# Nyström attention, feed-forward and top-1 experts on one core: another order of scores, sums and weights in the first batch

## The chip, the cores and the metric

The kernel runs on one core of a Trainium2 chip. The metric is the device time of one execution in microseconds (us). The core has five engines that run their own instruction streams in order: TensorE (PE, with its weight loads shown as PEld), VectorE (DVE), ScalarE (ACT), GpSimd (POOL) and SyncE (SP), whose queue issues nearly all DMAs. A change below 0.2% (some 2.5 us) can hardly be told from none.

## The reference, cut to what matters

```python
# q, k, v: (8, 8, 576, 64): 8 batches, 8 heads, 576 tokens; m = 32 landmarks, D = 64
q_lm = q.reshape(B, H, m, S // m, D).mean(axis=3)      # sums of 18 tokens
k_lm = k.reshape(B, H, m, S // m, D).mean(axis=3)
A  = sm(q, k_lm)          # sm: softmax of the scaled scores
Bm = sm(q_lm, k_lm)
C  = sm(q_lm, k)
Z  = Bm.transpose(0, 1, 3, 2) / (norm1 * norminf + 1e-06)
for _ in range(6):
    Z = 2 * Z - Z @ Bm @ Z
x = A @ Z @ C @ v                                      # then to (4608, 512)
h = np.maximum(x @ w_in, 0.0)                          # w_in 512 x 2048
x = (h * h) @ w_out                                    # w_out 2048 x 512
# then: logits, argmax, one of 8 experts for each token: relu(x @ w1[e]) @ w2[e], gated
```

## The kernel before

**Tiling.** A batch is 576 tokens, worked on in two halves of 288 (`c` = 0, 1). The attention's last factor Z·C·v is a matrix `wt` (128x128) of a batch, and instead of x the kernel forms G = wt · w_in (`gt`, tiles `gb`) in four rounds of 512 columns of w_in each (`chunk`, PE rows `bank<-wf,wt` or `two<-wf,wt`; `split_g` then makes a high and a low part, on ACT and DVE). `gemm(b)` runs for each half over 16 chunks `f` of the hidden layer: 6 matmuls `hp<-ab,gb` (128x288), then on ACT `r` = relu, `gh` = rounded square and `g` = square, on DVE `gl` = g - gh, and two chunks later (`second`) 12 matmuls `acc<-gh,wo` and `acc<-gl,wo`. Below, (0,0) is batch 0's first half, (0,1) its second, (1,0) batch 1's first half.

**Side work.** While `gemm(b)` runs, the attention of batch b+1 (`unit`: sums, transposes, landmarks, scores, softmax, powers of Z, wt) is woven between its matmuls at a rate from `RATES`. Batch 0's own unit (`u["early"]`) runs ahead of everything, with 8 of the weight pieces converted beside it. A scheduler sets the order of instructions in each queue from priorities; where the code says `follow`, an order is forced.

**Sums and landmarks.** Landmark sums (18 tokens each) are made from the loaded keys or queries `t`, four heads (`hg`) at a time. In batches 0 and 1 (`u["pe"]`) they are made on DVE (2 reduces), with a copy on POOL that doubles them, but batch 0's last group of queries is summed on POOL; in the other batches all is on POOL (`st`, `sums`). `landmarks` then transposes the doubled sums (128x128) on PE, two transposes for the keys and two for the queries of a batch.

**Weights.** w_in and w_out arrive as 8-byte floats, in 16 pieces each, 512 KB apiece (`raw`, SP's queue). A piece becomes 4-byte floats in steps: `m` (ACT for half of w_in's first pieces, POOL for the others), `r` (ACT), and two adds of halves on POOL (tiles `wf` for w_in, `w` for w_out). The order is all of w_in, then all of w_out. A w_in piece is also written back to memory (`win`), from where later batches read it (`wi`). A w_out piece is at once split into a high (ACT L218) and a low part (DVE L224) in its final tile `wo`; `w` has two buffers, so POOL's third piece waits for DVE's split of the first. The split cannot start before G has used the w_in piece, since `wo` takes over that piece's tile.

Of the kernel before, what the change touches and what calls it, by code (L numbers as in the profile page):

```python
# [23 lines left out]
LM = 32  # L24
# [16 lines left out]
CONV_BUFS = 2  # L41


CONV_EARLY = 14
CONV = 0.45
CONV_SOON = 0.8
CONV_FIRST = 2
# [5 lines left out]
RATES = {(0, 0): 0.3, (0, 1): 0.8}  # L53
# [4 lines left out]
G_STEPS = {7: 0, 10: 1, 13: 2, 15: 3}  # L58
# [34 lines left out]
class Kernel:  # L93
    def __init__(self, tc, ins, out):
# [7 lines left out]
        self.held = []  # L102
# [43 lines left out]
    def convert(self, jobs):  # L146
# [19 lines left out]
        def fetch(i):  # L166

            j, c = pieces[i]
            raw = pool.tile([128, 2 * W], I32, tag="raw", name="raw", bufs=RB)
            nc.sync.dma_start(  # L170
                out=raw.bitcast(U16)[:, 0:4 * W - 1], in_=jobs[j][0][:, c:c + W].bitcast(U16)[:, 1:4 * W]
            )
            st[i] = raw

        def scale(i):
# [56 lines left out]
    def convert_in(self):  # L232

        def job(i):
            n, kp = divmod(i, KD)

            def place():
                self.wf[i] = self.wop.tile([128, 2, 512], F32, tag=f"wo{i}", name="wf")[:, 0]
# [5 lines left out]
                lambda w: self.hold(lambda: self.nc.sync.dma_start(out=self.win_d[n][:, kp], in_=w)),  # L244
# [4 lines left out]
    def convert_out(self):  # L249

        def job(f):
            def parts(w):
                while self.g_done <= f // KD:
                    self.first_g_of(self.g_done)
                self.wo[f] = self.wop.tile([128, 2, DM], F32R, tag=f"wo{f}", name="wo")
                self.split(self.wo[f], w, self.nc.vector)

            return (
                self.w_out[f * 128:(f + 1) * 128, :],
                lambda: self.cv.tile([128, 512], F32, tag="cw", name="w", bufs=CONV_BUFS),  # L260
                parts,
# [3 lines left out]


# [150 lines left out]
    def load_next(self, pool=None):  # L417
# [7 lines left out]
        self.nc.sync.dma_start(  # L425
            out=t.rearrange("p s d -> p (s d)"), in_=src.rearrange("h (l s) d -> (h l) (s d)", s=SEG)
        )

    def load_v(self, b, g, pool=None):
        if b < B:  # L430
            t = self.vt[b, g] = (pool or self.ld).tile([PT, 4, R6 * D], F32, tag="v", name="v", bufs=1)
            src = self.v[b].rearrange("(a g i) (p r) d -> a g p i (r d)", g=2, i=2, r=R6)
            for a in range(2):
                self.nc.sync.dma_start(out=t[:, 2 * a:2 * a + 2], in_=src[a, g])

    def sums(self, u, nm, hg):

        if hg == 0:
            u[nm + "s"] = self.sm.tile([128, 2, 2, D], F32, tag=f"{nm}s", name="sums", bufs=1)
        s, t = u[nm + "s"][:, hg], self.qk[nm, u["b"], hg]  # L440
        if not u["pe"] or u["early"] and nm == "q" and hg == 1:
# [18 lines left out]
        self.nc.gpsimd.tensor_copy(out=s[:, 1], in_=s[:, 0])  # L460

    def transposed(self, u, nm, hg, i):

        if i == 0:
            u[nm, hg] = self.tp.tile([128, 4, 9, LM], F32, tag="xT", name="x", bufs=2)
# [11 lines left out]
        if i == 2 and not (u["b"] == 0 and nm == "q" and hg == 1):  # L477
            self.hold(self.load_next)
# [35 lines left out]
    def landmarks(self, u, nm):  # L514
        nc = self.nc
        pd = self.bank()
        with self.run_of():
            for hg in range(2):
                self.transpose(
                    pd[:, 128 * hg:128 * hg + 128], u[nm + "s"][:, hg].rearrange("p c d -> p (c d)"), self.ident  # L520
                )
# [272 lines left out]
    def last_values(self, u):  # L794
# [4 lines left out]
        for j in range(4):  # L799
            self.nc.vector.tensor_copy(out=self.crossed(wz, j), in_=w[32 * j:32 * j + 32])  # L800
# [26 lines left out]
    def unit(self, u):  # L827

        both = [(hg, i) for hg in range(2) for i in range(3)]
        if u["pe"]:  # L830
            self.sums(u, "k", 0)
            for hg, i in both:
                self.transposed(u, "k", hg, i)
                if (hg, i) == (0, 0):
                    self.sums(u, "k", 1)
                elif i == 2:
                    self.sums(u, "q", hg)
# [7 lines left out]
        for nm in "kq":  # L845
            self.landmarks(u, nm)
            yield STEP
# [35 lines left out]
        def a():  # L883
            yield STEP
            for i in range(2):
                self.scores_a(u, i)
                yield STEP
                yield STEP
# [677 lines left out]
```

## Time and profile before

| | us |
|---|---|
| median of 3 runs | 1260.96 |
| the runs | 1259.1 to 1261.58 |
| profiled execution | 1259.2 |
| its span | 1257.5 |
| PE busy | 1206.7 (96%) |
| DVE, ACT, POOL busy | 591.3, 615.2, 421.3 |

The profile is of one execution, 1.8 us below the median. It names for every instruction the line of the kernel (L402 is the helper that emits the big matmuls, L398 that for small ones, L410 transposes), the tile written and the tiles read. A window view gives how busy each engine was in a stretch and PEclk, the granted clock of TensorE as a share of its full speed (1.00 is 2.4 GHz, .50 is 1.2 GHz). Matmuls overlap in the timeline, so what one occupies is the distance from its start to the next one's start.

### The profile page before, as it was taken

The page shows a single profiled execution, that of the slowest core. Times are in us where ns is not written, and L with a number is a line of the kernel's source. Part 1 is how long each engine was busy: PE and PEld are TensorE (multiplying, and loading weights), DVE is VectorE, ACT ScalarE, POOL GpSimd, SP SyncE. Part 2 cuts the span into 40 slices and gives each one's busy share as a digit, 9 for nine tenths or more (in the row PEclk, how much of TensorE's full clock was granted, in tenths as well). Part 3 has the DMA queues.
Part 4 walks back from the last instruction along what each step waited for, and adds up shares of the span by engine and source line. Part 5 has one row for each costly group of instructions (what it writes and reads, how often), then busy time and mean ns, then how long its engine had stood idle before and what let it go on. Part 6 is the DMA issues. An engine that isn't in the chain of part 4 may idle for free.

```text
span 1257.5 us, 25149 instructions
## 1 busy us (share of the span) xinstructions
PE 1206.7 (96%) x9834; PEld 1078.6 (86%) x9834; DVE 591.3 (47%) x1498; ACT 615.2 (49%) x1433; POOL 421.3 (34%) x568
## 2 busy tenths in 40 slices
PE   4598999999999999999999999999999999999996
PEld 3377888989989989989989999998888888888885
DVE  5586466567547557556556332233333323323231
ACT  5586364564564564564564454553343433424331
POOL 5787514332233233232112000163342423424220
PEclk7699999999999999999999999999999999999998
DMA  9944333252152142141133210152534435343231
GB/s 339 336 164 135 124 122 109 91 168 61 59 171 64 53 158 77 53 158 58 54 120 108 69 37 2 39 151 84 143 105 139 129 115 159 108 125 110 90 96 40
DMA packets 88408, 142.24 MB, mean 113 GB/s; under 512 B 6430, under 2 KB 61758, under 8 KB 84702
## 3 DMA queue, kind: packets, MB, share of 16 engines
q1 hardware_dynamic: 87854, 139.97, 34.4%
q8 instruction: 79, 1.29, 0.4%
q0 software_dynamic: 288, 0.43, 0.1%
q14 instruction: 43, 0.35, 0.1%
q10 hardware_dynamic: 144, 0.20, 0.0%
HBM read 117.47 MB, written 23.11 MB: 112 GB/s over the span
## 4 chain that ended last, share of the span: by engine, by line
PE 90%; DVE 3%; DMA 3%; ACT 2%; POOL 1%; issue 1%; SPq 0%; POOLq 0%; ACTq 0%; DVEq 0%
PE acc L402 32%; PE hp L402 32%; PE y L402 17%; PE two L398 4%; PE bank L398 2%; PE bank L410 1%; DMA raw<-in_moe_w_in_dram 1%; PE pl L398 1%; DMA v<-in_v_dram 1%; PE pt L1168 1%; DVE x L488 1%; DMA t<-in_q_dram 1%; DVE gl L1079 1%; ACT r L185 0%; DVE ma L559 0%
## 5 line engine op out<-in xcount | busy, mean ns | idle before, releaser
L402 PE MATMUL acc<-gh,wo 128*128 128x288 f32 x2048 | 453.5, 299 | 7.7 <-ACT wo L218 5.0
L402 PEld LDWEIGHTS acc<-gh,wo 128*128 128x128 f32 x2048 | 341.1, 189 | 30.0 <-ACT gh L1077 8.4
L402 PE MATMUL acc<-gl,wo 128*128 128x288 f32 x1024 | 288.9, 298 | 1.1 <-DVE gl L1079 1.1
L402 PE MATMUL hp<-ab,gb 128*128 128x288 f32 x1536 | 255.7, 301 | 1.6 <-ACT r L1076 1.5
L402 PEld LDWEIGHTS hp<-ab,gb 128*128 128x128 f32 x1536 | 216.0, 189 | 21.3 <-issue 11.8
L1076 ACT ACTIVATE r<-hp 128x288 f32<-128x288 f32 x256 | 105.4, 412 | 256.0 <-PE hp L402 254.4
L1079 DVE TENSOR_TENSOR gl<-g,gh 128x288 fp32r<-128x288 f32 x256 | 131.4, 514 | 198.8 <-ACT g L1078 192.6
L402 PE MATMUL y<-s,h 128*128 128x512 f32 (+1 forms) x896 | 223.0, 396 | 0.8 <-ACT h L1311 0.5
L402 PEld LDWEIGHTS hp<-xs,s 128*128 128x128 f32 x1536 | 212.2, 188 | 7.5 <-DVE ls L1522 0.3
L402 PE MATMUL hp<-xs,s 128*128 128x288 f32 x1536 | 217.1, 295 | 0.2 <-DVE ls L1522 0.2
L402 PEld LDWEIGHTS acc<-gl,wo 128*128 128x128 f32 x1024 | 193.4, 189 | 4.0 <-DVE gl L1079 3.0
L402 PEld LDWEIGHTS y<-s,h 128*128 128x128 f32 (+1 forms) x896 | 160.6, 184 | 37.7 <-ACT h L1311 0.7
L230 POOL TENSOR_TENSOR s<-r,s 128x256 fp32r<-128x256 f32 x128 | 102.0, 819 | 234.8 <-ACT s L218 234.8
L1311 ACT ACTIVATE h<-hp 128x288 fp32r<-128x288 f32 x128 | 52.6, 412 | 186.8 <-PE hp L402 172.6
L1314 DVE SCALAR_TENSOR_TENSOR h<-hp,h 128x64 fp32r<-128x64 f32 (+2 forms) x192 | 62.6, 354 | 166.3 <-ACT h L1311 165.9
L1077 ACT ACTIVATE gh<-r 128x288 fp32r<-128x288 f32 x256 | 114.2, 446 | 12.5 <-PE acc L402 5.8
L1078 ACT ACTIVATE g<-r 128x288 f32<-128x288 f32 x256 | 110.6, 432 | 5.3 <-DVE gl L1079 5.0
L218 ACT CAST s<-r 128x512 fp32r<-128x512 f32 x128 | 77.6, 617 | 71.4 <-PE y L402 56.1
L499 POOL COPY x<-x 32x576 f32<-32x576 f32 x48 | 33.9, 706 | 195.7 <-DVE x L488 102.7
L224 DVE TENSOR_TENSOR s<-r,s 128x512 fp32r<-128x512 f32 x64 | 50.9, 795 | 103.3 <-ACT s L218 103.3
L230 POOL TENSOR_TENSOR xs<-xr,xs 128x576 fp32r<-128x576 f32 x32 | 45.9, 1459 | 64.0 <-ACT xs L218 48.0
L444 POOL TENSOR_TENSOR st<-t 128x288 f32<-128x288 f32 x50 | 40.7, 835 | 75.1 <-DMA t<-in_q_dram 73.1
(198 smaller groups left out, 1097.7 us busy)
## 6 DMA issues: line engine op xcount, KB each, us to landing
r<-in_moe_w_dram SPq DMA_DIRECT2D x128, 256.0 KB
wi<-win SPq DMA_DIRECT2D x28, 1024.0 KB
t<-in_k_dram SPq DMA_DIRECT2D x16, 576.0 KB
t<-in_q_dram SPq DMA_DIRECT2D x16, 576.0 KB
v<-in_v_dram SPq DMA_DIRECT2D x32, 288.0 KB
x_d<-x SPq DMA_DIRECT2D x16, 576.0 KB
xr<-x_d SPq DMA_DIRECT2D x16, 576.0 KB
raw<-in_moe_w_in_dram SPq DMA_DIRECT2D x16, 511.8 KB
```

The source lines that it names most:

```text
L218: hi = self.nc.scalar.copy(out=t[:, 0], in_=raw)
L224: lo_eng.tensor_tensor(out=t[:, 1], in0=raw, in1=t[:, 0].bitcast(F32), op=ALU.subtract)
L230: self.nc.gpsimd.tensor_tensor(out=out[:, p], in0=in0[:, p], in1=in1[:, p], op=op)
L398: self.in_run(lambda: self.nc.tensor.matmul(out, **kw))
L402: mm = self.nc.tensor.matmul(out, **kw)
L444: add = lambda out, in0, in1: self.nc.gpsimd.tensor_tensor(out=out, in0=in0, in1=in1, op=ALU.add)
L1076: nc.scalar.activation(out=r, in_=hp[:, 0:HC], func=ACTF.Relu)
L1077: nc.scalar.activation(out=gh, in_=r, func=ACTF.Square)
L1078: nc.scalar.activation(out=g2, in_=r, func=ACTF.Square)
L1079: nc.vector.tensor_tensor(out=gl, in0=g2, in1=gh.bitcast(F32), op=ALU.subtract)
L1311: nc.scalar.activation(out=h[:, t0:t1], in_=hp[:, 0:HC], func=ACTF.Relu)
L1314: nc.vector.scalar_tensor_tensor(out=h[:, to + a:to + z], in0=hp[:, a - t0:z - t0], scalar=0.0, in1=h[:, a:z].bitcast(F32), op0=ALU.max, o ...
```

## The change

- The early unit (batch 0) makes all sums on VectorE, transposes keys and queries first, then takes the key landmarks, A's scores, the query landmarks and C's scores. Two of its four `wz` copies go to ScalarE.
- In all batches the sums are no longer doubled: `landmarks` multiplies the 64-column sums with the identity twice, into the upper and the lower 64 partitions (four 64x128 matmuls in place of two 128x128 transposes), and POOL's copies are gone.
- Batch 1's `k` (both groups) and first `q` are loaded behind batch 0's `v` and summed at three steps of the prologue (`SUMS_AT`). Batch 0's `v` now comes behind eight pieces of w_in.
- The weights' order is 8 pieces of w_in, 2 of w_out, then one of each in turn. `CONV_BUFS` is 3, ACT makes `m` of 12 pieces (8 before). Whole w_out pieces stay in tiles of their own (`wb`), and `split_out` splits them when `gemm` comes to them; the high part goes into the tile of the w_in piece of the same number (`wa`), so it also comes behind that piece's write to `win`. These writes are now held back behind the loads (`paced`).
- In (0,0) `g2` is made on DVE, and the last two rounds of batch 0's G come at f = 0 and 4. Rates: .35 for (0,0), .5 for (0,1). Batch 1's G: round 0 at the end of (0,1), rounds 1 to 3 at f = 2, 6, 10 of (1,0), before at f = 7, 10, 13, 15 of (0,1).

```diff
-CONV_BUFS = 2
+CONV_BUFS = 3
-CONV_EARLY = 14
+CONV_EARLY = 13
+SUMS_AT = {26: ("k", 0), 30: ("k", 1), 34: ("q", 0)}
-RATES = {(0, 0): 0.3, (0, 1): 0.8}
+RATES = {(0, 0): 0.35, (0, 1): 0.5}
-G_STEPS = {7: 0, 10: 1, 13: 2, 15: 3}
+G_STEPS = {(1, 7): 0, (1, 10): 1, (1, 13): 2, (1, 15): 3}
+G_LATER = {(1, 15): 0, (2, 2): 1, (2, 6): 2, (2, 10): 3}
...
-            if i < 4 * KD and i % 2 == 0:
-                nc.scalar.activation(out=top, in_=high, func=ACTF.Copy)
+            if jobs[i][3] and i % 2 == 0:
+                ops.append(nc.scalar.activation(out=top, in_=high, func=ACTF.Copy))
...
-                lambda w: self.hold(lambda: self.nc.sync.dma_start(out=self.win_d[n][:, kp], in_=w)),
+                lambda w: self.hold(lambda: self.paced(self.nc.sync.dma_start(out=self.win_d[n][:, kp], in_=w))),
...
+    def weights_order(self):
+        i, o = self.convert_in(), self.convert_out()
+        first, rest = i[:G_FIRST * KD], i[G_FIRST * KD:]
+        jobs = first + o[:2]
+        for k, w in enumerate(rest):
+            jobs += [w, o[2 + k]]
+        return jobs + o[2 + len(rest):]
+
+    def split_out(self, last):
+        while len(self.wo) <= min(last, NFC - 1):
+            f = len(self.wo)
+            while f not in self.whole:
+                next(self.conv)
+            while self.g_done <= f // KD:
+                self.first_g_of(self.g_done)
+            w = self.whole[f]
+            hi = self.wop.tile([128, 512], F32R, tag=f"wa{f}", name="hi")
+            lo = self.wop.tile([128, 512], F32R, tag=f"wb{f}", name="lo")
+            self.nc.scalar.copy(out=hi, in_=w)
+            self.nc.vector.tensor_tensor(out=lo, in0=w, in1=hi.bitcast(F32), op=ALU.subtract)
+            self.wo[f] = hi, lo
...
-        if not u["pe"] or u["early"] and nm == "q" and hg == 1:
+        if not u["pe"]:
...
-        self.nc.gpsimd.tensor_copy(out=s[:, 1], in_=s[:, 0])
...
             for hg in range(2):
-                self.transpose(
-                    pd[:, 128 * hg:128 * hg + 128], u[nm + "s"][:, hg].rearrange("p c d -> p (c d)"), self.ident
-                )
+                for c in (1, 0):
+                    self.matmul(
+                        pd[64 * c:64 * c + 64, 128 * hg:128 * hg + 128], lhsT=u[nm + "s"][:, hg], rhs=self.ident,
+                        start=True, stop=True,
+                    )
...
+            if self.ahead is None and len(self.raws) >= G_FIRST * KD and i >= 12:
+                self.pacer = self.raws[G_FIRST * KD - 1]
+                self.load_v(0, 0)
+                self.load_v(0, 1, early)
+                for _ in range(3):
+                    self.load_next()
+                self.ahead = self.unit_of(1)
+            if self.ahead is not None and i in SUMS_AT:
+                self.sums(self.ahead, *SUMS_AT[i])
...
-                if (b, c) == (0, 0) and f > 0 and f % 2 == 0 and self.g_done < min(4, f // 2 + G_FIRST):
+                if (b, c) == (0, 0) and f % 4 == 0 and self.g_done < min(4, f // 4 + G_FIRST):
                     self.first_g_of(self.g_done)
+                if (b, c) == (0, 0):
+                    self.split_out(f)
...
-                    nc.scalar.activation(out=g2, in_=r, func=ACTF.Square)
+                    if (b, c) == (0, 0):
+                        nc.vector.tensor_tensor(out=g2, in0=r, in1=r, op=ALU.mult)
+                    else:
+                        nc.scalar.activation(out=g2, in_=r, func=ACTF.Square)
...
-                if last is None and c == 1 and f in G_STEPS:
-                    self.next_g(b + 1, G_STEPS[f])
+                if last is None and (c, f) in (G_STEPS if b else G_LATER):
+                    self.next_g(b + 1, (G_STEPS if b else G_LATER)[c, f])
+                elif (b, c) == (1, 0) and (2, f) in G_LATER:
+                    self.next_g(b, G_LATER[2, f])
```

How instructions stand on the engines that the prediction speaks of (tiles as above; the number after x is how many stand in a row):

SP, from its first instruction on, before: the loads of batch 0 and the first weights.

```order
L425 DMA t<-in_k_dram 128x1152 x2
L425 DMA t<-in_q_dram 128x1152 x2
L170 DMA raw<-in_moe_w_in_dram 128x2047 x3
L434 DMA v<-in_v_dram 96x2x384 x4
L170 DMA raw<-in_moe_w_in_dram 128x2047
L425 DMA t<-in_k_dram 128x1152 x2
L170 DMA raw<-in_moe_w_in_dram 128x2047
L244 DMA win_112<-wf 128x512
L170 DMA raw<-in_moe_w_in_dram 128x2047 x2
```

SP at the same place after:

```order
L447 DMA t<-in_k_dram 128x1152 x2
L447 DMA t<-in_q_dram 128x1152 x2
L172 DMA raw<-in_moe_w_in_dram 128x2047 x8
L461 DMA v<-in_v_dram 96x2x384 x2
L172 DMA raw<-in_moe_w_out_dram 128x2047
L461 DMA v<-in_v_dram 96x2x384 x2
L447 DMA t<-in_k_dram 128x1152
L172 DMA raw<-in_moe_w_out_dram 128x2047
L447 DMA t<-in_k_dram 128x1152
L447 DMA t<-in_q_dram 128x1152
L172 DMA raw<-in_moe_w_in_dram 128x2047
```

All eight first pieces now stand ahead of `v`, batch 1's keys and queries behind it, and no write of `win` stands among them; the writes come behind the piece of number 21.

POOL, from the middle of w_out's conversion on, before (`st` is the sum of batch 2's keys, `w<-m,r` a piece of w_out, `m<-raw` its cast):

```order
L184 CAST m<-raw 128x512 x2
L230 TENSOR_TENSOR w<-m,r 128x256 x2
L444 TENSOR_TENSOR st<-t 128x288 x2
L230 TENSOR_TENSOR w<-m,r 128x256 x2
L184 CAST m<-raw 128x512
L444 TENSOR_TENSOR st<-st 128x256
L184 CAST m<-raw 128x512
L230 TENSOR_TENSOR w<-m,r 128x256 x2
L444 TENSOR_TENSOR st<-st 128x128
L230 TENSOR_TENSOR w<-m,r 128x256 x2
```

POOL where w_out's first pieces are made, after:

```order
L233 TENSOR_TENSOR w<-m,r 128x256 x2
L187 CAST m<-raw 128x512 x2
L233 TENSOR_TENSOR wf<-m,r 128x256 x2
L233 TENSOR_TENSOR w<-m,r 128x256 x4
L187 CAST m<-raw 128x512
L233 TENSOR_TENSOR wf<-m,r 128x256 x4
L233 TENSOR_TENSOR w<-m,r 128x256 x2
L187 CAST m<-raw 128x512 x2
L233 TENSOR_TENSOR wf<-m,r 128x256 x2
L233 TENSOR_TENSOR w<-m,r 128x256 x4
```

The sums of batch 2 no longer stand between the pieces, and pieces of w_in (`wf`) and w_out (`w`) take turns from the first on.

ACT around the first chunk of (0,0), before (`wo<-w` the high part of a w_out piece, `gb` a round of G, `r<-hp` and `gh` the first chunk):

```order
L185 ACTIVATE r<-raw 128x512 x3
L218 CAST wo<-w 128x512
L1019 CAST gb<-two 128x512
L473 COPY x<-bank 128x3x4x32
L185 ACTIVATE r<-raw 128x512
L1076 ACTIVATE r<-hp 128x288
L1077 ACTIVATE gh<-r 128x288
L1078 ACTIVATE g_806<-r 128x288
```

ACT at the same place after:

```order
L188 ACTIVATE r<-raw 128x512 x2
L185 ACTIVATE m<-raw 128x512
L188 ACTIVATE r<-raw 128x512
L1130 ACTIVATE r<-hp 128x288
L285 CAST hi<-w 128x512 x2
L1131 ACTIVATE gh<-r 128x288
L285 CAST hi<-w 128x512 x2
L502 COPY x<-bank 128x3x4x32
L1071 CAST gb<-two 128x512
```

Ahead of the first `gh` two high parts stand where one stood, behind it two more, and the `g` of the chunk is gone.

PE while batch 3 is in `gemm`, before, where a landmark of batch 4 is transposed:

```order
L402 MATMUL acc<-gh,wo 128x288
L410 MATMUL bank<-ident,sums 128x128 x2
L402 MATMUL hp<-ab,gb 128x288 x6
L402 MATMUL acc<-gh,wo 128x288 x4
L402 MATMUL acc<-gl,wo 128x288
```

PE where the first group of the same landmark stands after:

```order
L424 MATMUL acc<-gh,hi 128x288 x4
L420 MATMUL bank<-ident,sums 64x128 x2
L424 MATMUL acc<-gl,hi 128x288
L424 MATMUL acc<-gh,lo 128x288
L424 MATMUL acc<-gl,hi 128x288
```

Two 64x128 matmuls stand where both groups' transposes stood, and the second group has another such place further on. Of the 12 landmarks of batches 2 to 7 ten are split into two places in this way and two stand whole (four matmuls in a row); of batch 1 one is whole and one split.

## Rows read from the trace of the kernel before

**Rows 1.** Page, busy time: engine, us, share of the span, instructions.

```profile
PE 1206.7 (96%) x9834; PEld 1078.6 (86%) x9834; DVE 591.3 (47%) x1498; ACT 615.2 (49%) x1433; POOL 421.3 (34%) x568
```

**Rows 2.** Chain of waits, 40 to 50 us: start us, duration us, what.

```profile
40.73 8.39 DMA raw<-in_moe_w_in_dram
...
49.23 0.78 ACT m L182
```

**Rows 3.** Groups by form, 0 to 55 us; columns as in the page's part 5.

```profile
L455 DVE TENSOR_REDUCE sums<-t 128x32 f32<-128x576 f32 x6 | 6.4, 1134 | 0.3 <-DMA t<-in_k_dram 0.3
...
L410 PE MATMUL bank<-ident,sums 128*128 128x128 f32 x4 | 1.6, 388 | 7.7 <-POOL sums L444 5.1 <-POOL sums L460 2.6
```

**Rows 4.** Timeline of DVE at 46.74 us: start, duration, what, [idle before <-releaser].

```profile
46.74 0.75 DVE L567 TENSOR_REDUCE ma<-aa 128x18 f32<-128x576 f32 x1 [2.35 <-ACT aa L565]
```

**Rows 5.** Timeline of PE, 50 to 56 us.

```profile
50.71 3.67 PE L398 MATMUL bank<-wf,wt 64*32 64x512 f32 x32 [0.89 <-ACT wt L816]
...
55.80 0.40 PE L402 MATMUL hp<-ab,gb 128*128 128x288 f32 x1
```

**Rows 6.** Windows, 20 to 50 us: PE, PEld, DVE, ACT, POOL busy, PEclk, DMA, GB/s.

```profile
20.00:30.00 10.00, 6.09 (x100) 4.84 (x96) 6.34 (x28) 8.51 (x23) 5.28 (x8) 0.59 1.06 397
30.00:40.00 10.00, 8.24 (x210) 4.44 (x198) 2.99 (x11) 5.48 (x12) 7.30 (x11) 0.75 1.02 345
40.00:50.00 10.00, 3.38 (x92) 2.48 (x84) 7.42 (x21) 5.22 (x10) 7.29 (x10) 0.50 1.05 352
```

**Rows 7.** Windows, 50 to 140 us, with their sum.

```profile
50.00:60.00 10.00, 6.71 (x57) 2.33 (x57) 6.17 (x8) 5.87 (x13) 9.42 (x14) 0.67 0.88 312
60.00:70.00 10.00, 8.97 (x57) 7.22 (x58) 9.31 (x12) 7.30 (x19) 7.13 (x13) 0.71 0.68 252
...
120.00:130.00 10.00, 5.47 (x37) 4.84 (x36) 9.68 (x17) 4.48 (x10) 8.47 (x13) 1.00 0.22 73
...
sum 90.00, PE 76.55 PEld 62.53 DVE 63.23 ACT 61.46 POOL 74.26; mean PE 8.51 PEld 6.95 DVE 7.03 ACT 6.83 POOL 8.25
```

**Rows 8.** Groups by form, 55 to 135 us.

```profile
L402 PE MATMUL acc<-gh,wo 128*128 128x288 f32 x140 | 33.9, 323 | 7.7 <-ACT wo L218 5.0 <-DVE wo L224 2.6
L230 POOL TENSOR_TENSOR w<-m,r 128x256 int32<-128x256 int32 x32 | 25.0, 805 | 6.8 <-DVE wo L224 6.8
...
L184 POOL CAST m<-raw 128x512 f16<-128x512 bf16 x17 | 14.9, 895 | 0.1
...
L1079 DVE TENSOR_TENSOR gl<-g,gh 128x288 fp32r<-128x288 f32 x19 | 12.0, 634 | 5.4 <-ACT gh L1077 3.6 <-ACT g L1078 1.6
...
L1078 ACT ACTIVATE g<-r 128x288 f32<-128x288 f32 x21 | 9.3, 445 | 5.3 <-DVE gl L1079 5.0
```

**Rows 9.** Timeline of PE, 331.7 to 332.9 us, steady state.

```profile
331.73 0.29 PE L402 MATMUL acc<-gh,wo 128*128 128x288 f32 x1
331.87 0.38 PE L410 MATMUL bank<-ident,sums 128*128 128x128 f32 x2
332.00 1.03 PE L402 MATMUL hp<-ab,gb 128*128 128x288 f32 x6
332.87 0.70 PE L402 MATMUL acc<-gh,wo 128*128 128x288 f32 x4
```

**Rows 10.** Timeline of PE, 328.1 to 329.3 us, steady state.

```profile
328.14 0.29 PE L402 MATMUL acc<-gh,wo 128*128 128x288 f32 x1
328.36 0.69 PE L398 MATMUL pl<-x,wg 128*32 128x288 f32 x8
328.99 0.40 PE L402 MATMUL acc<-gh,wo 128*128 128x288 f32 x1
329.22 0.29 PE L402 MATMUL acc<-gl,wo 128*128 128x288 f32 x1
```

**Rows 11.** Timeline of PE, 220.8 to 221.2 us, steady state.

```profile
220.83 0.58 PE L398 MATMUL bank<-eu,dg 128*128 128x96 f32 x4
221.19 0.38 PE L402 MATMUL acc<-gl,wo 128*128 128x288 f32 x1
```

More of the change, by code (lines that the diff above doesn't have):

```diff
@@ L237, in place @@
             def place():
-                self.wf[i] = self.wop.tile([128, 2, 512], F32, tag=f"wo{i}", name="wf")[:, 0]
+                self.wf[i] = self.wop.tile([128, 512], F32, tag=f"wa{i}", name="wf")
                 return self.wf[i]
@@ L251, in job @@
         def job(f):
[L252 to L256, printed above, removed]
             return (
                 self.w_out[f * 128:(f + 1) * 128, :],
-                lambda: self.cv.tile([128, 512], F32, tag="cw", name="w", bufs=CONV_BUFS),
-                parts,
+                lambda: self.wop.tile([128, 512], F32, tag=f"wb{f + 1}", name="w"),
+                lambda w: self.whole.update({f: w}),
+                False,
             )
         return [job(f) for f in range(NFC)]
+    def weights_order(self):
[18 more added lines that the diff above has]
+            self.wo[f] = hi, lo
     def run(self):
@@ L433, in load_v @@
             for a in range(2):
-                self.nc.sync.dma_start(out=t[:, 2 * a:2 * a + 2], in_=src[a, g])
+                op = self.nc.sync.dma_start(out=t[:, 2 * a:2 * a + 2], in_=src[a, g])
+                self.paced(op)
+                if b == 0:
+                    self.pacer = op
     def sums(self, u, nm, hg):
-        if hg == 0:
-            u[nm + "s"] = self.sm.tile([128, 2, 2, D], F32, tag=f"{nm}s", name="sums", bufs=1)
+        if nm + "s" not in u:
+            u[nm + "s"] = self.sm.tile([128, 2, D], F32, tag=f"{nm}s", name="sums", bufs=1)
         s, t = u[nm + "s"][:, hg], self.qk[nm, u["b"], hg]
-        if not u["pe"] or u["early"] and nm == "q" and hg == 1:
+        if not u["pe"]:
             t = t.rearrange("p s d -> p (s d)")
@@ L829, in unit @@
         both = [(hg, i) for hg in range(2) for i in range(3)]
-        if u["pe"]:
-            self.sums(u, "k", 0)
+        if u["early"]:
+            for nm, hg in (("k", 0), ("k", 1), ("q", 0), ("q", 1)):
+                self.sums(u, nm, hg)
+            for nm in "kq":
+                for hg, i in both:
+                    self.transposed(u, nm, hg, i)
+                    yield STEP
+        elif u["pe"]:
             for hg, i in both:
                 self.transposed(u, "k", hg, i)
[L834 to L837, printed above, removed]
+                if (hg, i) == (1, 0):
+                    self.sums(u, "q", 1)
                 yield STEP
@@ L844, in unit, with a_scores @@
                 yield STEP
-        for nm in "kq":
-            self.landmarks(u, nm)
-            yield STEP
+        def a_scores():
+            for i in range(2):
+                self.scores_a(u, i)
+                yield STEP
+                yield STEP
+        self.landmarks(u, "k")
+        yield STEP
+        if u["early"]:
+            yield from a_scores()
+        self.landmarks(u, "q")
+        yield STEP
         def sc():
@@ L884, in a @@
             yield STEP
[L885 to L888, printed above, removed]
+            if not u["early"]:
+                yield from a_scores()
             yield from weave(self.softmax_a(u, 0), self.softmax_a(u, 1))
@@ L905, in unit @@
             yield from weave(sc(), self.softmax_b(u))
-            yield from weave(self.sooner(weave(cv_alone(), self.powers(u))), itertools.chain(tq(), a()))
+            yield from weave(self.sooner(weave(cv_alone(), self.powers(u))), a())
             with self.tc.high_priority(100):
@@ L1025, in all_steps @@
         for b in range(1, B):
-            yield from self.unit(self.unit_of(b))
+            yield from self.unit(self.ahead if b == 1 else self.unit_of(b))
     def load_at(self, b, c):
@@ L1099, in second @@
         nc = self.nc
-        while f not in self.wo:
-            next(self.conv)
+        self.split_out(f)
         if f == 0:
```

44 lines of the change are left out of this document (25 added, 19 removed).

## The prediction

> **What bounds the kernel now.** I read the page's busy times first: PE works 1206.7 us of a span of 1257.5 [rows 1], so 50.8 us are open to an order of work, and anything that lengthens PE's own work adds to the end one for one. Then the windows. From 20 to 50 us PE is busy 6.1, 8.2 and 3.4 us in ten, at a granted clock of .59, .75 and .50 [rows 6], that is for most of the time at the lower of its two levels, after stretches in which it waited. From 50 to 140 us it is busy 76.55 of 90 [rows 7]: 13.45 us idle, and 6.71 + 8.97 us of busy time at clocks of .67 and .71, which full speed would do in 4.5 + 6.4, so 4.8 us more. The two losses are 18.2 us. After that the profile's waits name nothing big, and the kernel is PE's own work. So three places are to be priced: the start to the first `hp`, the stretch in which weights are still converted, and the steady state, where seven batches each take the new landmarks.
>
> **The start.** Four things change on the way to `wt`, G and the first `hp`, which starts at 55.80 [rows 5].
> - Sums of batch 0. PE waited 5.1 us for POOL's sum of the last queries [rows 3]. All eight reduces go to DVE, and the key landmarks and A's scores stand ahead of the query landmarks: -5.1.
> - A's softmax is in DVE's queue earlier. Before, DVE waited 2.35 us for ACT's `aa` with the `wz` copies queued behind [rows 4]: -2.4. The `wz` copies divided between DVE and ACT: nothing taken.
> - Weights. The chain of waits runs over the DMAs, the last over a w_in piece that came at 49.1, whose `m` and `r` stood ahead of `wt` on ACT [rows 2]; PE waited 0.89 for `wt` [rows 5]. Now the eight pieces stand ahead of `v` on SP. Their 4.2 MB and the 2.4 MB of keys and queries, at the 345 to 397 GB/s of rows 6, are in by about 20 us: -0.9. What is late next is the chain of powers.
> - Batch 1's sums. Six reduces, 6.4 us by the same six in rows 3, now stand in DVE's queue between the powers' steps, and `ef`, `ee` and PE wait behind them. DVE was busy 63%, 30% and 74% there [rows 6]; the busy share, 56% on average, is what I take as not hidden: +3.6.
> The sum is **-4.8**. Bounds: +3.1 if the wait of 5.1 was not on the path and the sums are wholly on it (-2.4 - 0.9 + 6.4); -8.4 if the sums are hidden.
>
> **The conversion stretch, 50 to 140 us.** PE's `acc` matmuls waited 5.0 us for ACT's high part and 2.6 for DVE's low part of w_out, and POOL 6.8 us for DVE to free `w` [rows 8]. These form a ring: POOL's next piece waits for the split of the one before, and the split for G. The change cuts it: pieces have tiles of their own, and w_out is begun right after w_in's eighth piece. POOL then never waits for a split. The whole 7.6 us of PE goes: -7.6. Idle time at 120 to 130 us is 4.53 with DVE busy 9.68 of 10 [rows 7]. DVE loses there batch 1's sums and three rounds of G, which go to the prologue and to (1,0), and takes 16 `g2`. The nearest row for a square of 128x288 is `gl`, 634 ns [rows 8]: 10.1 us, spread over the first half only. I take half of the idle time: -2.3. Fewer waits also mean less time at the low clock, half of the 4.8: -2.4. The sum is **-12.3**, with bounds 0 (each wait comes back as another) and -18.2 (nothing is lost at all).
> What covers this is ACT. It was busy 61.5 of 90 [rows 7]. It loses 16 `g` of 445 ns [rows 8], 7.1 us, and gets four `m` of 780 ns [rows 2], 3.1 us, so there is room, but in its queue the first `gh` stands behind two high parts (before: one). POOL loses four casts of 895 ns [rows 8] and seven small copies, and batch 2's sums move behind w_out; nothing needs them before batch 2's landmarks in (1,0), so that costs nothing; if POOL were late there, the landmarks would wait and `gemm` go on. SP's 16 writes of `win`, moved past the loads, are wanted back only for batch 1's G at the end of (0,1): nothing, but for the high parts (rival 4).
>
> **The landmarks.** In steady state two transposes of sums and six `hp` take 332.87 - 331.87 = 1.00 us, and a 288-column matmul 0.13 to 0.14 (331.73 to 331.87) [rows 9], so the pair takes 1.00 - 6 x 0.13 = 0.21. The new pair is two plain 4-byte matmuls of 64 columns' width, each 128 columns long. Two rows bear on it. Two plain 4-byte matmuls of 96 columns (four in the trace, which counts each twice) occupy 0.36 [rows 11], which is 0.24 for one of 128 and 0.54 for one of 288. And `pl`, four such of 288 side by side in groups of 32 columns, occupies from the end of the matmul before, 328.27, to 0.13 before 329.22, that is 0.82 [rows 10]: side by side they cost 0.54, and going to the narrow shape and back 0.28. A pair then costs 0.24 + 0.28 = 0.52. A split landmark has two pairs in place of 0.21, one of which replaces each half: +0.41 a pair; a whole one is 0.48 + 0.28 - 0.21 = +0.55. Batches 1 to 7 have 22 pairs and 3 whole ones: 22 x 0.41 + 3 x 0.55 = **+10.7**. All of it is PE's own time and nothing hides it. Bounds: without the 0.28, 22 x 0.13 + 3 x 0.27 = +3.7; one after another and not side by side, 22 x (0.48 + 0.28 - 0.105) + 3 x (0.96 + 0.28 - 0.21) = +17.5. I take the middle, since `pl` is the same kind, type and neighbourhood. Batch 0's two landmarks lie on the start and exchange copies on POOL for longer matmuls: nothing taken.
> The Trainium skill, TensorEngine Tiling (Array Packing), Theoretical Speedup, gives up to a factor of two for a dimension of at most 64; by that alone the sum here would be the +3.7 above. The same page, Key Properties, says that a change of tiling mode drains TensorE; by that a pair pays at both ends, and the `pl` row, with its 0.28, agrees.
>
> **Three rounds of G in (1,0).** They are the same matmuls at another place. The first of them and the `wt` transposed right ahead of it stand with `hp` behind: exposed are the wait for `wt`, 0.89 [rows 5], and part of a round's split on ACT and DVE. I take **+1.3**, bounds 0 and 2.2 (the wait and twice a `gl`).
>
> **The sum.** -4.8 - 12.3 + 10.7 + 1.3 = -5.1 against the profiled execution of 1259.2: 1254.1. The median of the runs is 1.8 higher, so 1255.9.
>
> **The rivals.**
> 1. *The narrow landmarks are cheap*: +3.7 in place of +10.7, so 1248.9. For it: `two<-wi,wt` and `two<-x,lm`, also narrow, stand beside some of the pairs, so that some changes of shape are shared. Against it: `pl` in the same neighbourhood, 0.82. 0.20.
> 2. *They run one after another*: +17.5, so 1262.7. For it: both halves read the same weights' columns and the same identity, where `pl` has other data. Against it: the output halves lie in different column groups, as `pl`'s do. 0.10.
> 3. *Nothing comes of the start*: batch 1's sums sit wholly in the powers' chain and the wait of 5.1 was covered by others: +3.1 in place of -4.8, so 1263.8. DVE's 74% at 40 to 50 us [rows 6] speak for it. 0.10.
> 4. *The high parts wait for the writes of `win`* (the one that ends slower). `hi` of chunk 0 takes the tile of w_in piece 0, whose write SP issues only behind piece 21, and that is issued when a `raw` buffer comes free, after the conversion of 17 pieces. POOL needs for a piece 1.6 us of adds (805 ns, twice) and for each one without ACT's `m` 0.9 more [rows 8]; pieces 8 to 17 take 5 x 1.6 + 5 x 2.5 = 20.5 us. If piece 8 starts at 32 us, that is at 53, and a write of 256 KB takes 0.8 us at 345 GB/s: in time for the first `r` at some 56 to 59 us, with little to spare. If conversion lags by 10 us, ACT stands at `hi`, behind it the first `gh`, behind it PE: the stretch's -12.3 becomes about +2, and the time is 1270. It decides from 5 us of lag on. For it: ACT, which makes each piece's `r` and often its `m`, was busy 8.5 of 10 us at 20 to 30 [rows 6]; against it, the first eight `raw` come sooner. 0.12.
>
> **How the numbers follow.** The forecast, near 1255.9, has 0.48; the rivals the chances above. The likeliest time is **1255.9**. The range goes down to rival 1 with a start at its better bound (1248.9 - 3.6 = 1245.3), and up past rivals 2 and 3 to 1266, half-way into rival 4: 1244 to 1266 leaves out about 2 in 10. Within 0.2%, about what a measurement of this kernel can tell from no change, is 1258.4 to 1263.5. Faster: all of rival 1 and 0.40 of the forecast, 0.60. Same: rivals 2 and 3 mostly and the rest of the forecast, 0.22. Slower: rival 4 and the outer part of 2 and 3, 0.18.
>
> **What would show it.** Right: the first `hp` at about 51 us; no wait of `acc` on `hi` or `lo` over 1 us; PE idle from 50 to 140 us under 8 us; a pair of sums that occupies some 0.5 us in steady state, and a batch some 1.5 us longer than before. Wrong: `hi` idle behind a DMA, reduces of batch 1 named as releasers of PE before 50 us, pairs at 0.25 or 0.75 us, or a new idle stretch of PE where (1,0) begins.

## The result and the profile after

The changed kernel takes 1277.05 us (median of 4 runs, 1276.27 to 1277.66) against 1261.27 of before (4 runs); the ratio is 1.0128, with a 95% interval of 1.011 to 1.0145. The prediction was 1255.9, faster: wrong in sign and outside its range. The profiled execution took 1277.26, its span is 1275.6 us, 18.1 more than before.

The page's busy row after, which answers to [rows 1] (engine, busy us, share of the span, instructions):

```profile
PE 1224.7 (96%) x9930; PEld 1086.9 (85%) x9930; DVE 603.9 (47%) x1514; ACT 617.0 (48%) x1423; POOL 407.7 (32%) x552
```

PE is busy 18.0 us longer, and the open 50.8 us of before are 50.9 now. So the loss is time in which PE works, not time in which it waits. To see where it lies I cut the span at the first `hp` of batches 0, 1, 2 and 7. Windows between these cuts, before and then after (us; length; PE, PEld, DVE, ACT, POOL busy; PEclk, DMA share, GB/s):

```profile
55.80:172.59 116.79, 104.05 (x918) 91.16 (x910) 75.69 (x154) 74.33 (x179) 73.82 (x102) 0.96 0.42 147
172.59:271.75 99.16, 98.60 (x939) 88.04 (x932) 65.81 (x171) 56.67 (x143) 32.13 (x49) 1.00 0.31 104
271.75:748.02 476.27, 475.69 (x4425) 431.14 (x4424) 265.50 (x712) 255.47 (x646) 125.21 (x188) 1.00 0.27 91
```

```profile
53.61:170.82 117.21, 106.50 (x902) 94.09 (x900) 77.53 (x150) 70.98 (x162) 63.00 (x83) 0.94 0.47 164
170.82:272.76 101.94, 100.74 (x945) 86.65 (x945) 59.32 (x152) 54.79 (x136) 31.18 (x49) 1.00 0.36 124
272.76:765.17 492.41, 490.74 (x4521) 436.88 (x4514) 273.55 (x743) 262.21 (x660) 126.55 (x198) 1.00 0.26 88
```

| stage | before | after | difference | predicted |
|---|---|---|---|---|
| to the first `hp` | 55.8 | 53.6 | -2.2 | -4.8 |
| gemm of batches 0 and 1 | 216.0 | 219.1 | +3.2 | -11.0 and landmarks |
| gemm of batches 2 to 6 | 476.3 | 492.4 | +16.1 | landmarks alone |
| from batch 7's gemm to the end | 509.5 | 510.4 | +1.0 | 0 |

In the first gemm PE idles 117.21 - 106.50 = 10.7 us, before 12.7; and at a mean clock of .94 in place of .96 its 106.5 us of busy time lose some 6.4 us against full speed, before 4.2 (an estimate from the two columns). What fewer waits gave, the lower clock took. From batch 2's gemm on PE waits for 1.7 us of 492 and is simply longer at work: 15 pairs and one whole landmark at the prices measured below make 7.5 of the 16.1 us, and 8.7 remain.

The waits that were to go have gone. After, from 50 to 172 us (engine and line, waited for: total us, times, longest):

```profile
PE hp L424 <- ACT r L1130: 4.8, 1, 4.8
PE acc L424 <- DVE gl L1136: 1.9, 3, 0.8
PE acc L424 <- ACT gh L1131: 0.9, 1, 0.9
PE two L420 <- DVE gb L1072: 0.8, 1, 0.8
```

No `acc` waits for a high or low part of w_out any more (7.6 us in [rows 8]); other releasers stand in their place, the largest of them new. It is the same ahead of the first `hp`: the 5.1 us for POOL's sums [rows 3] are gone, but the wait for ACT's `ec` has grown. Before:

```profile
PE bank L410 <- ACT ec L595: 3.2, 1, 3.2
```

After (`ee` is a step of the powers of Z):

```profile
PE bank L432 <- ACT ec L627: 7.2, 1, 7.2
PE bank L420 <- DVE ee L805: 6.5, 3, 4.6
```

PE idles 25.4 us of the 53.6 to the first `hp`, before 25.9 of 55.8.

### The profile page after: what moved, and what is told of

Same layout as the page of the kernel before. It is cut to its first block, busy times and chain, and to the rows that moved or that the text cites. A ratio compares the mean times of both kernels' runs of the same rounds, so it can differ in the third digit from the quotient of the medians.

```text
span 1275.6 us, 25301 instructions
## 1 busy us (share of the span) xinstructions
PE 1224.7 (96%) x9930; PEld 1086.9 (85%) x9930; DVE 603.9 (47%) x1514; ACT 617.0 (48%) x1423; POOL 407.7 (32%) x552
## 4 chain that ended last, share of the span: by engine, by line
PE 88%; DVE 6%; DMA 2%; ACT 2%; issue 1%; POOL 0%; SPq 0%; POOLq 0%; DVEq 0%; ACTq 0%
PE hp L424 31%; PE acc L424 30%; PE y L424 16%; PE two L420 4%; PE bank L420 3%; PE bank L432 1%; DMA t<-in_k_dram 1%; DVE x L518 1%; PE pl L420 1%; DVE gl L1136 1%; PE pt L1227 1%; DMA win<-wf 1%; DVE sums L484 1%; DVE x L522 1%; DVE ma L591 0%
## 5 line engine op out<-in xcount | busy, mean ns | idle before, releaser
L424 PE MATMUL acc<-gl,hi 128*128 128x288 f32 x1024 | 289.8, 301 | 3.6 <-DVE gl L1136 3.4
L424 PE MATMUL acc<-gh,lo 128*128 128x288 f32 x1024 | 284.7, 297 | 0.0
L424 PE MATMUL hp<-ab,gb 128*128 128x288 f32 x1536 | 260.1, 304 | 6.9 <-ACT r L1130 5.1
L424 PEld LDWEIGHTS hp<-ab,gb 128*128 128x128 f32 x1536 | 216.5, 189 | 39.2 <-issue 18.1
L1136 DVE TENSOR_TENSOR gl<-g,gh 128x288 fp32r<-128x288 f32 x256 | 134.6, 527 | 236.4 <-ACT g L1135 232.7
L424 PE MATMUL acc<-gh,hi 128*128 128x288 f32 x1024 | 209.2, 301 | 0.9 <-ACT gh L1131 0.9
L424 PEld LDWEIGHTS acc<-gl,hi 128*128 128x128 f32 x1024 | 193.7, 189 | 13.8 <-DVE gl L1136 5.8
L424 PEld LDWEIGHTS acc<-gh,lo 128*128 128x128 f32 x1024 | 193.2, 189 | 1.3 <-issue 1.3
L424 PEld LDWEIGHTS acc<-gh,hi 128*128 128x128 f32 x1024 | 159.3, 189 | 13.5 <-ACT gh L1131 7.1
L1135 ACT ACTIVATE g<-r 128x288 f32<-128x288 f32 x240 | 103.0, 429 | 0.0
L227 DVE TENSOR_TENSOR s<-r,s 128x512 fp32r<-128x512 f32 x64 | 50.8, 793 | 102.8 <-ACT s L221 102.8
```

What stands on the lines that cost most here:

```text
L227: lo_eng.tensor_tensor(out=t[:, 1], in0=raw, in1=t[:, 0].bitcast(F32), op=ALU.subtract)
L424: mm = self.nc.tensor.matmul(out, **kw)
L1135: nc.scalar.activation(out=g2, in_=r, func=ACTF.Square)
L1136: nc.vector.tensor_tensor(out=gl, in0=g2, in1=gh.bitcast(F32), op=ALU.subtract)
```

## The experiments

Two theories stood at the beginning. A: the narrow landmark matmuls cost PE's own time, as predicted, and somewhat more of it. B: the side work (the next batch's attention) runs later in the batch than before and in smaller groups, which costs more on PE whatever the landmarks are. Every variant is compared with the kernel before, run beside it on the same chip; the ratio of after to it is 1.0128. Where a variant is set against after, the difference of the two medians is given; by the two ratios each variant of after comes out up to 2 us slower than that.

**1. The landmarks alone, taken out of after and put into before.**

```diff
# a_oldlm: after, landmarks of before;  b_newlm: before, with the opposite edit
-                for c in (1, 0):
-                    self.matmul(pd[64 * c:64 * c + 64, ...], lhsT=u[nm + "s"][:, hg], rhs=self.ident, ...)
+                self.transpose(pd[:, 128 * hg:128 * hg + 128], u[nm + "s"][:, hg]..., self.ident)
...
+        self.nc.gpsimd.tensor_copy(out=s[:, 1], in_=s[:, 0])
```

> The changed kernel with the landmarks of before in all batches (doubled sums, two 128x128 transposes; POOL's copies are back). Theory A (the narrow matmuls cost PE's own time): each pair in the trace of after takes 0.57 us against 0.11 for the transpose it replaces, 22 pairs and 3 whole ones make 11.7 us, so 1265 us. Theory B (the loss is side work that now runs later and in smaller groups): the time stays above 1272 us.

> The kernel before with nothing but the new landmarks (single sums, four 64x128 matmuls, no copies on POOL). Theory A: +11 to +12 us, 1273 us. Theory B: +4 us at most, 1265 us.

After with the old landmarks: 1265.99, ratio 1.0047 (1.003 to 1.0064), so 11 us less (10.2 by the ratios), as A says. Before with the new landmarks: 1260.1, ratio 1.0003 (.9993 to 1.0013), no change, which A does not say. Both are read on PE's timeline. In after, a pair (start us, us, what; x4 since a plain 4-byte matmul is listed twice):

```profile
455.47 0.30 PE L424 MATMUL acc<-gh,lo 128*128 128x288 f32 x1
455.70 0.44 PE L420 MATMUL bank<-ident,sums 128*64 128x128 f32 x4
456.07 0.80 PE L424 MATMUL hp<-ab,gb 128*128 128x288 f32 x4
```

The `acc` is done streaming at about 455.60 (its start and 0.13), the next matmul starts at 456.07, and the one after it not 0.13 but 0.24 later: 0.47 + 0.11, with the starts of the single instructions 0.57 us a pair. In before with the new landmarks, where all four matmuls stand together:

```profile
426.33 0.29 PE L402 MATMUL acc<-gh,wo 128*128 128x288 f32 x1
426.56 0.66 PE L398 MATMUL bank<-ident,sums 128*64 128x128 f32 x8
427.14 0.92 PE L402 MATMUL hp<-ab,gb 128*128 128x288 f32 x5
```

From 426.46 to 427.14 are 0.68, with the same 0.11 behind 0.79 us for a whole landmark, against 0.22 for the two transposes. So whole it costs 0.57 more, split in two 2 x 0.57 - 0.22 = 0.92 more. After has 22 pairs and 3 whole ones in batches 1 to 7: 22 x 0.46 + 3 x 0.57 = 11.8 us, about what a_oldlm gained; in batches 2 to 6, where PE hardly waits, it is 7.5 us by the sum and 7.4 by the windows (485.0 in place of 492.4).

In b_newlm all 14 are whole, 8.0 us. Against this, the landmark's small products now stand in one group with the scores behind them, 0.94 us in place of 0.45 + 0.84, 0.35 less a batch; and the first gemm, which with both should be 0.8 us longer, is 3.4 shorter (113.4), with PE idle for 9.8 us in place of 12.7. That leaves some 1.3 us; its span is 0.5 us longer than that of before, and the other 0.8 stays open.

**2. The gain without the loss.** POOL's copies are only in batches 0 and 1, where DVE makes the sums; in the others POOL doubles them in its last add.

```diff
# b_hybrid: before, with
-        self.nc.gpsimd.tensor_copy(out=s[:, 1], in_=s[:, 0])
+                if u["pe"] and not (u["early"] and nm == "q" and hg == 1):
+                    # the two 64x128 matmuls, else the transpose
```

> The kernel before with the new landmarks only where VectorE makes the sums (batches 0 and 1), so that POOL's seven copies go; batches 2 to 7 keep the transposes of doubled sums. If the new landmarks alone broke even because the first batches gained what batches 3 to 7 lost (first gemm 3.4 us shorter, batches 3 to 5 some 0.5 us longer each), this keeps the gain without the loss: 3 us faster than before, 1257. If the gain in the first gemm came from another order and not from the copies: within 1 us of before.

1256.33, ratio .9974 (.9962 to .9985): 3 us faster than before. First gemm 114.6 us in place of 116.8, batches 2 to 6 at 476.3 as before.

**3. Rates and places of G.** After with the old landmarks still takes 485.0 us for batches 2 to 6, 8.7 more than before, so there is a loss that has nothing to do with them.

```diff
# a_oldrate: after, with        b_rates: before, with the opposite first edit
-RATES = {(0, 0): 0.35, (0, 1): 0.5}
+RATES = {(0, 0): 0.3, (0, 1): 0.8}
# a_oldrate, and a_gsteps alone
-G_LATER = {(1, 15): 0, (2, 2): 1, (2, 6): 2, (2, 10): 3}
+G_LATER = G_STEPS
```

> The changed kernel with the rates of before (.3 in (0,0), .8 in (0,1)) and all four rounds of batch 1's G back in (0,1). Theory A: within 2 us of after, 1275 to 1279. Theory B: the side work is done earlier again and batch 6 carries less of it, 1271 to 1273.

> The kernel before with the two rates of after alone (.35 in (0,0), .5 in (0,1)). After loses 8.7 us from the third batch's gemm on that the landmarks do not explain, and lost them too with the old landmarks (gemm of batches 2 to 6: 476.3 us before, 485.0 in that run). If the cause is that the side work then runs half a batch later and its narrow matmuls stand in more, smaller groups: gemms 3 to 5 rise from 95.4 to 97 us or more, 1264 to 1268 us. Rival: the loss comes from the moved rounds of G or from the sums, and the rates alone stay within 2 us of before.

> The changed kernel with all four rounds of batch 1's G back in (0,1), the rates as in after. With the rates undone as well it took 1271. If the rounds of G are what moved the side work: 1271 to 1273. If the rates: 1276 to 1278.

a_oldrate: 1271.1, ratio 1.0088 (1.0071 to 1.0105). a_gsteps: 1278.44, ratio 1.0145 (1.0128 to 1.0162), its interval overlaps that of after: the places of G show no effect. b_rates: 1267.4, ratio 1.0056 (1.0039 to 1.0073): two numbers cost the kernel before 7.5 us. Its windows show where, in the third stage, 8.0 us longer than before's:

```profile
272.09:756.35 484.26, 482.24 (x4447) 433.83 (x4446) 272.92 (x725) 260.35 (x654) 124.48 (x192) 1.00 0.27 90
```

The two rates, lower together, leave the attention behind for good: in gemms 3 to 5 the small products of the landmarks stand 60 us behind the gemm's first `hp` in before and 77 us in b_rates (in after they come in the next gemm, 3 to 11 us behind its first `hp`), and meet other neighbours. One group of scores in before, 16 rows of `two<-x,lm` in one piece:

```profile
374.29 0.55 PE L402 MATMUL hp<-ab,gb 128*128 128x288 f32 x3
374.77 0.72 PE L398 MATMUL two<-x,lm 64*32 64x288 f32 x16
375.41 0.54 PE L402 MATMUL acc<-gh,wo 128*128 128x288 f32 x2
```

The same group in b_rates, in two pieces of 4 and 12:

```profile
480.74 0.56 PE L402 MATMUL acc<-gh,wo 128*128 128x288 f32 x3
481.23 0.68 PE L398 MATMUL two<-x,lm 64*32 64x288 f32 x4
481.83 0.40 PE L402 MATMUL acc<-gl,wo 128*128 128x288 f32 x1
482.07 0.29 PE L402 MATMUL acc<-gh,wo 128*128 128x288 f32 x1
```

```profile
485.51 0.29 PE L402 MATMUL acc<-gh,wo 128*128 128x288 f32 x1
485.73 0.70 PE L398 MATMUL two<-x,lm 64*32 64x288 f32 x12
486.36 0.40 PE L402 MATMUL acc<-gl,wo 128*128 128x288 f32 x1
486.60 0.29 PE L402 MATMUL acc<-gh,wo 128*128 128x288 f32 x1
```

From the first of the narrow matmuls to the next wide one it is 0.64, 0.60 and 0.63 us: four narrow matmuls take nearly as long as sixteen, and the second piece's whole time is lost, 0.8 us with the delay behind it. Each of the gemms of batches 2 to 6 has one such split, other small groups have other neighbours, and the gemms of batches 3 to 5 take 97.0 to 97.1 us, before 95.4 to 95.5: 4.9 of the 8.0 us. Each of these three gemms has the same 576 wide and 317 listed small matmuls in both kernels; at 0.13 us for a wide one, the small ones and the delays around them take 22.2 us in place of 20.6, at 27 places in place of 26, and half of this difference is the split. The other 3.1 are batch 6's gemm, 95.0 in place of 90.1, less 1.7 that batch 2's is shorter: side work that before did in the first two gemms (160 rows of `two<-x,lm` there, 144 in b_rates), which are as long without it.

**4. Batch 1's early sums.**

```diff
# a_noahead: after, with
-SUMS_AT = {26: ("k", 0), 30: ("k", 1), 34: ("q", 0)}
+SUMS_AT = {}
...
         elif u["pe"]:
+            for nm, hg in (("k", 0), ("k", 1), ("q", 0)):
+                self.sums(u, nm, hg)
```

> The changed kernel with batch 1's keys and first queries loaded early as in after, but summed only when batch 1's attention begins. If the reduces in DVE's queue (a wait of 3.6 us for the DMA and 6.6 us of work, between the powers) hold the start, the first hp comes at 45 to 48 us in place of 53.6 and the time falls by 4 to 6 us, to 1272. Rival: ACT, which waits for pieces of weights from 57 to 61 us, holds the first acc at 65 us anyway, and the time stays within 2 us of 1277.

1272.03, ratio 1.0092 (1.0076 to 1.0109), with runs from 1270.2 to 1275.2. The profiled one is the longest of these; in it the first `hp` comes at 52.06, 1.5 us earlier than in after. This comparison is loose: three other kernels with the same instructions on each engine up to there as after (a_gsteps, a_g2act, a_oldrate) start at 55.60, 55.76 and 55.14, so after's 53.61 is the best of four. DVE's queue in after says why the sums cost anything (start us, us, what, [idle before <-releaser]):

```profile
29.50 0.23 DVE L809 TENSOR_TENSOR ef<-i,ee 128x64 f32<-128x64 f32 x1
33.37 2.14 DVE L484 TENSOR_REDUCE sums<-t 128x32 f32<-128x576 f32 x2 [3.63 <-DMA t<-in_k_dram]
...
36.27 0.21 DVE L805 COPY ee<-bank 128x64 f32<-128x64 f32 x1
36.41 2.18 DVE L484 TENSOR_REDUCE sums<-t 128x32 f32<-128x576 f32 x2
...
38.63 0.22 DVE L813 TENSOR_TENSOR ef<-ef,bank 128x64 f32<-128x64 f32 x1
38.76 2.29 DVE L484 TENSOR_REDUCE sums<-t 128x32 f32<-128x576 f32 x2
```

The powers' next step, `ee` at 36.27, stood behind a reduce whose keys landed at 33.3 us, and later steps behind two more. Without the sums DVE's first `wz` copy starts at 41.56 in place of 45.93; but PE then waits 3.64 us for ACT's `wz` copies, which stand behind pieces of the weights (in after 2.3; in before 3.64 for DVE's).

**5. What holds the first gemm.**

```diff
# a_worder: after, with
+        return i + o                      # all of w_in, then all of w_out
# a_winfree: after, with
-   self.hold(lambda: self.paced(self.nc.sync.dma_start(out=self.win_d[n][:, kp], in_=w)))
+   self.hold(lambda: self.nc.sync.dma_start(out=self.win_d[n][:, kp], in_=w))
# a_g2act: after, with g2 on ScalarE in (0,0) too
# a_early10: after, with
-CONV_EARLY = 13
+CONV_EARLY = 10
```

> The changed kernel with all of w_in ahead of all of w_out, as in before. If the early w_out pieces and tiles of their own are what the stretch from 50 to 140 us gained, the high parts are late again and PE waits for them: 1283 us or more. If the supply of w_out was not what held PE (ACT was, with the pieces' r and m ahead of the first chunks): within 3 us of 1277, or faster.

> The changed kernel with the writes of w_in's pieces no longer forced behind the loads (they go out when a piece is ready, as in before). In after nine writes left together at 55.5 us, and ACT then waited 3.1 us for a raw piece of w_out and 1.0 us for a write. If that DMA burst holds the first chunks, the first acc comes some 3 us earlier and the time is 1273 to 1274. Rival: the writes then share the loads' bandwidth before 35 us, batch 1's keys land later, DVE waits longer for them, and the time is 1277 to 1281.

> The changed kernel with (0,0)'s 16 squares g2 back on ScalarE. If ACT is what PE waits for in (0,0) (hp waited 4.8 us for ACT's r), 16 x 445 ns come back on it: 1281 to 1284. If DVE is as late (16 squares took 11.3 us there): within 2 us of 1277.

> The changed kernel with CONV_EARLY 10 in place of 13: since w_in and w_out take turns there, each w_in piece less is a w_out piece less whose m and r stand in ACT's queue ahead of the first chunk. In after PE waited 4.8 us for ACT's r of the first chunk, which stood behind an r of a raw piece that came late (3.1 us). If that queue is what took the gain of the first gemm: this wait falls under 1.5 us and the time by 3 us or more, to 1274 or less. If the gain goes on to another wait (w_out's high parts, DVE): within 2 us of 1277 with about 10 us of PE idle in the first gemm as before.

a_worder: 1272.18, ratio 1.0103 (1.0086 to 1.012). The order that was to feed w_out early cost 3 to 5 us (by the ratios, by the medians), not gained 7.6. Its first gemm:

```profile
54.97:166.28 111.31, 99.77 (x895) 88.71 (x887) 77.93 (x148) 66.19 (x155) 68.45 (x86) 0.98 0.49 173
```

It is 5.9 us shorter than after's at a mean clock of .98, with as much idle time (11.5), though it begins 1.4 us later; its `acc` waits for high and low parts again, 4.3 us, and other waits are shorter.

a_winfree: 1277.02, ratio 1.0139 (1.0122 to 1.0156), nothing: the waits for `r` and for the write are gone from its trace, and `acc` waits 6.1 us for DVE's `gl` in their place, in after 1.9. a_g2act: 1276.82, ratio 1.0133 (1.0116 to 1.015), nothing: which of the two engines makes these squares makes no difference here. a_early10: 1274.34, ratio 1.011 (1.0093 to 1.0127), some 2.7 us less than after. It was to shorten the queue that held the first chunk in after. PE in after, and ACT:

```profile
53.61 1.06 PE L424 MATMUL hp<-ab,gb 128*128 128x288 f32 x6
...
62.41 1.81 PE L424 MATMUL hp<-ab,gb 128*128 128x288 f32 x6 [4.82 <-ACT r L1130]
65.07 1.33 PE L424 MATMUL acc<-gh,hi 128*128 128x288 f32 x4 [0.85 <-ACT gh L1131]
```

```profile
57.56 0.78 ACT L185 ACTIVATE m<-raw 128x512 f16<-128x512 bf16 x1
61.40 0.66 ACT L188 ACTIVATE r<-raw 128x512 int32<-128x512 uint32 x1 [3.06 <-DMA raw<-in_moe_w_out_dram]
61.97 0.39 ACT L1130 ACTIVATE r<-hp 128x288 f32<-128x288 f32 x1
63.39 1.28 ACT L285 CAST hi<-w 128x512 fp32r<-128x512 f32 x2 [1.03 <-DMA win<-wf]
64.58 0.44 ACT L1131 ACTIVATE gh<-r 128x288 fp32r<-128x288 f32 x1
```

The first `hp` was done by 54.7, but its `r` on ACT came at 61.97, behind an `r` of a piece of w_out that arrived late; `gh` then stood behind two high parts, as the order had shown. In a_early10 the wait shrinks and another takes its place:

```profile
PE two L420 <- DVE gb L1072: 4.5, 1, 4.5
PE hp L424 <- ACT r L1130: 2.9, 2, 2.1
```

**6. All four costly parts undone.**

```diff
# a_mix4: after, with the edits of 2 (landmarks), 3 (rates and G), 4 and a_worder
# a_mix3: a_mix4 without the edit of 4;  a_mix4_early: a_mix4 with CONV_EARLY = 11
```

> The changed kernel with four parts undone: new landmarks only where VectorE makes the sums, old rates and places of G, batch 1's sums when its attention begins, all of w_in ahead of w_out. What is left is the early unit's order and sums, the loads' order, tiles of their own for w_out, g2 on DVE. If the losses add up (-11, -6, -5, -5 against after): 1250, faster than before by 0.7%. If they overlap (the same wait of PE in the first gemm taken away several times): 1257 to 1260.

> As the kernel with four parts undone, but batch 1's sums stay early on DVE between the powers. If they hold the start: 2 to 5 us longer than that kernel, with the first hp some 1.5 us or more later. If not: the same within 1 us.

> The kernel with four parts undone and CONV_EARLY 11. There the w_out pieces come last, so that only two w_in pieces leave ACT's queue ahead of the first chunk. If ACT's queue holds it: 1249 to 1250. If the conversion's own length does (POOL and ACT need the same work for 32 pieces either way): 1251 to 1253.

a_mix4: 1251.81, ratio .9937 (.9921 to .9954), faster than both kernels: 25 us less than after, where the four undone one by one gave 27: the losses add up nearly in full. a_mix3: 1254.18, ratio .9962 (.9948 to .9977). Their first `hp`:

```profile
49.87 1.06 PE L420 MATMUL hp<-ab,gb 128*128 128x288 f32 x6
```

```profile
54.40 1.06 PE L420 MATMUL hp<-ab,gb 128*128 128x288 f32 x6
```

In these two profiles 4.5 us of the start hang on batch 1's early sums; the medians differ by 2.4. a_mix4_early, which I expected at 1253 or less, took 1257.72, ratio .9976 (.9967 to .9986): fewer pieces converted ahead of the first chunk cost 5 to 6 us. In its trace G and the high parts are late:

```profile
PE bank L428 <- DVE gb L1076: 4.0, 1, 4.0
PE hp L420 <- ACT r L1134: 3.7, 4, 1.2
PE acc L420 <- ACT hi L281: 2.8, 3, 1.5
```

## Why the prediction was wrong, point by point

Between the two profiles the forecast of -5.1 missed by 23 us: some 10 in the conversion stretch with G, 9 in batches 2 to 6 beside the landmarks, 3 at the start, 1 by the landmarks and 1 from batch 7's gemm on.

**The start, -4.8: -2.2 at best.** After's 53.61 is the best of four starts of the same instructions, whose mean is 55.0, 0.8 earlier than before. The price of the sums, +3.6, is borne out in size: 4.5 us of start between a_mix3 and a_mix4, 1.5 between after and a_noahead, and 2.4 and 5.0 of the whole time. It came in part by a wait that has no term, 3.6 us of DVE for batch 1's keys. The failed step is the gain without them, -8.4: that each of three waits would go in full. Without the sums the first `hp` comes 5.9 us earlier than before in a_mix4, where three other parts are undone too, and 3.7 in a_noahead. The wait of 5.1 went, but that for ACT's `ec` grew from 3.2 to 7.2. PE's wait for `wz`, 3.64 before, is 2.3 in after and 3.64 again in a_noahead, for ACT's copies. How much of each lies on the path was not separated.

**The conversion stretch, -12.3: about -1.** Both batches' gemms together are 3.2 us longer; 4.4 of that are their seven pairs and two whole landmarks (G's three rounds, +1.3 forecast, are in it too). The step that failed is "the whole 7.6 us of PE goes". The waits did go, and PE idled almost as long for others. I named ACT as the cover, with room by its busy sum; a sum over 90 us does not show that ACT stands still for 3.1 us behind one late piece while the first chunk waits behind it. The other step is the half of the slow clock, -2.4: it was paid back with 2.2 more. And the order of weights itself was a loss, 3 to 5 us in a_worder. PE idles 9.2 to 13.5 us in the first gemm of all these kernels, whichever wait an edit takes away; which one would have to go for it to shrink was not found and stays open.

**The landmarks, +10.7: +11.8.** Right, by the sum of the pairs in the trace, and again by a_oldlm (-11). The price of a pair, +0.41, was 0.46; of a whole one, +0.55, 0.57. (The two transposes are 1.00 - 6 x 0.13 = 0.22, not the 0.21 of the prediction.) Rivals 1 and 2 are out: not 0.25, not 0.76, but 0.57 for a pair. On the Trainium skill's page TensorEngine Tiling (Array Packing), Key Properties, a change of mode drains TensorE; the pairs agree, with 0.57 us in all, where a second pair right behind adds only 0.22. Its Theoretical Speedup, up to a factor of two for a dimension of at most 64, shows in this 0.22, against 0.24 for one such matmul alone (the prediction's estimate from [rows 11]), and not in the total.

**What had no term: the rates, +8.7 in batches 2 to 6.** This is the other failed step. The change names them, and the prediction prices only the moved rounds of G; the rates stand at nothing, without a reason. They set the phase of all later batches: 7.5 us by b_rates, nearly all of it in gemms that the two rates do not name. In after 4.9 of the 8.7 us go with the rates (batches 2 to 6 take 487.5 us in a_oldrate, 492.4 in after); what the rest is, among the other things that shift the phase (sums, landmarks, G), was not separated.

**Three rounds of G, +1.3.** By a_gsteps the move made the kernel 1.4 us faster, if anything, which is not to be told from nothing: the term is not borne out, and it is small.

**Rival 4** (high parts wait for `win`) took place at 1.0 us and did not matter: in a_winfree the wait is gone and the time the same. **Rival 3**, nothing from the start (+3.1), was about as far from the start's mean of -0.8 as the forecast.

## What to carry to other kernels

Where PE is the bound, look at every step that is pushed into its stream for how often it changes the shape of the matmuls, and count the places and not the instructions: here four narrow matmuls cost nearly what sixteen cost. A number that paces side work at the beginning may set its phase for the whole run, so compare the groups of a late batch in the two orders even if the code touches only the first. And here waits that were removed in front of in-order queues came back as others, at the start and in the first gemm, so walk the whole stretch before you price one; a busy sum of the covering engine is no proof of cover.

## What the runs showed of the hardware that I had not expected

A visit to a narrow shape costs at both ends. The wide matmul before one is followed after 0.22 to 0.23 us (455.47 to 455.70), before a transpose after 0.13 to 0.14 [rows 9]. The first wide matmul behind one is followed after 0.24 (481.83 to 482.07); behind transposes it is 0.21 to 0.22, so this part is not the narrow shape's alone. A group of 4, 12 or 16 narrow matmuls of 288 columns occupies 0.80, 0.83 and 0.84 us with both. And PE's granted clock in the first gemm, .94 to .98, moved the time more than its waits did: by the estimate above 6.4 us lost in after and 2.0 in a_worder, at 10.7 and 11.5 us of idle time.
